# A gated linear attention with a feed-forward block on one core: the written-out order of five instruction queues is replaced by another

## The chip, the cores and the metric

One core of a Trainium2 chip runs the whole program in one launch. The metric is device time in microseconds (us), the median of several runs of the same program. TensorE (PE), VectorE (DVE), ScalarE (ACT), GpSimd (POOL) and SyncE (SP) each work through a queue of their own in order; an instruction whose inputs are not there yet holds up everything behind it on its engine. SP does no arithmetic here: it only issues DMA transfers. POOL computes and issues DMA transfers too.

## The reference

Inputs q, k, v and f_logit are float32, (4 batches, 8 heads, 768 tokens, 48). For each batch and head a 48x48 state is carried over the tokens:

```
f = 1 / (1 + exp(-f_logit))
state = f[t][:, None] * state + outer(k[t], v[t])
y[t]  = q[t] @ state
```

Then, with x = y as 3072 tokens x 384: h = x @ w_in (384 x 2048), g = 0.5 * (h + sqrt(h*h + 4)), out = g @ w_out (2048 x 384).

## The kernel before, in words

The 3072 tokens are cut into 24 **rows** of 128 tokens (r0 to r23; six rows a batch), and two rows make a **pair** (p0 to p11). Pairs 0 to 2 are loaded and prepared row by row (`FINE`), the others pair by pair. Each piece of work is an operation (`P.add`) with a letter in `TAKE` and a queue name in `NAME`:

- **Loads (SP, L315):** F, Q, K, V bring f_logit, q, k, v of a row (192 KB, one DMA) or of a pair (two DMAs).
- **Weights (POOL, L339):** w_in in eight parts, w_out in eight parts (192 KB each), in the order 0 to 7.
- **Logarithms (`add_logs`):** ACT takes exp (L360) and ln (L365) of F; "hi" (L368) and "lo" (L371) split the result into two fp16 tiles, on DVE or POOL.
- **Decays (`add_decays`):** PE makes the cumulative sums ("W", L402 to L409) in PSUM tiles `hps`; ACT takes ea and eap (L416); "q-mul" and "k-mul" (L422) give the decayed q and k, "v" (L429) is a cast, each on DVE or POOL; nls (L436, L438, DVE) and gam (L475, ACT) give the row's total decay.
- **Attention (`add_attention`), row by row:** q and k are transposed, for rows 0 to 9 on PE (T, L524) with a copy by DVE or ACT (L528), from row 10 on by a DMA transpose that SP issues ("xq", L512). Then the scores (SC, L549), the mask on DVE (pm, L556), the state (KV, L634 and L637, its copy sn on DVE, L641), the output (Y, L570 and L572), its copy (Yc, L579 on ACT or L581 on DVE), and the transpose of y into xT, on PE for rows 0 to 9 (YT, L614, L617) and by DMA from row 10 on ("xy", L604).
- **Feed-forward (`add_mlp1`, `add_mlp2`), pair by pair:** M1 (L671) is an eighth of h for one pair: six matmuls into one `hps` tile, for which both xT halves and one w_in part are needed; M1 of pair 6, part 3 is written M1 6.3. ACT squares it (L677) and takes one root for two parts (L686); DVE makes g (L694). M2 (L713) is a quarter of one row's output: four matmuls. The output tile is copied ("ev", L722 on ACT, L724 on DVE) and stored ("out", L728) from POOL or SP.

**What sets the order.** `TAKE` holds one string for each engine: the order in which that engine takes from its queues (each queue in its own order). `ENG` says, place by place, which engine does the operations that two engines can do: D for DVE, P for POOL, A for ACT, S for SP. `Plan.run` only merges the five strings into one program order. So the strings fix the whole schedule on each engine, and a wait at the head of a queue is a wait for all behind it.

Buffers that bind: five PSUM tiles `hps` (`NH`), shared in turn by M1, W and, in the first rows, attention. So an M1 part can't start before the g of the part five tiles back has been made. ACT changes its function table between the exp/ln work and the root (L761, L763), 12 loads in all. Load buffers: three for F, four each for Q, K, V.

Of the kernel before, what the change touches and what calls it, by code (L numbers as in the profile page):

```python
# [23 lines left out]
}  # L24
TAKE = {
    "PE":
        "WWTSTWSWYKTSYTKtStKYWYWttT11SK1K1Y1111T1t1S11211Y1t11122W2112222TT2K11S222YWW2t21S22T1TY22t2K11S112K"
        "1Y1Kt1122WS22WS22YY2t2K11S112YK22K211112S211211Y211S2112Y2WSW2KY2222S111KY12K222S112112YK112S112S11Y"
        "2211Y22SW2W22211212KY1K2211S211YK211S1122Y11S11K2222Y111S12222Y11211222111122221112122222222222",
    "ACT":  # L30
        "WWWWWWWWWWTWWWWWWWWcWWWWcWWWWWWmWmrmmrmmrmmrmmrmmrmmrmmrmmrWWWWWWWmmrmmrWWWWmWWWWWmrmmrmmrmcmrmmrWWW"
        "WWWWWmWmrmmrmmrmmrmmrmmrmmrmmrWWWWWWWWWmWmrmmrmmrmmrcmmrmmermmcrmmcrWWWWmWmrmmremmrmmrcmmrmmremmmmrr"
        "cemmmmrrecmmrmmrmmrmmremmmrmreee",
    "DVE":
        "hlvknnlSTSSnKnkSThSSTKStKStcckknntTtKSSggcKgghggTtgSggSggcgtgggggegkenTTlKhSSgggegckntnSSTeTcthKggSg"
        "SKggegKgtgggSSeSSccntKneSScKgggeKggSggSgggcegSgSggcgSSecgnKnSSeKKcggeggSSggKggSSgSggSgggeggSSknenKcg"
        "gKgSSgggKggSSggcggSKSggggSSgggggggeggggggggg",
    "POOL":
        "hlkkkhhvlvkkkvhiivlliiiiikkviuuuluuuuuvkholookkhvvolklkovvkoohkkhoollkkkkvhoohvlvlkkkovoo",
    "SP":  # L40
        "VFFFQHQVHFVQHHHFQFHVQQVVFQFFVVHHFFQQQVFHHHFqqVVHHqyyQqQQqqyFFyVqoqyVyqVqQHoyyQoqHqyyooVqyqyoyyoooo",
}

ENG = {
    "hi": "DPPPDPDPPPDPDPPPPPPPPPP",
    "lo": "DPDPPPPPDPPPPPPPPPPPPPP",
    "qk": "PPPDPPPDDDPPDPPPDPPPPPPPPPPPPPPPPPPPPPPPDPPPPP",
    "v16": "DPPPPPPPPPPPPPPPPPPPPPP",
    "T": "ADDDDDDDDDDDDDDDDDDDDDDD",
    "Yc": "AADDDDDDADDDDDDDAAADADAA",  # L50
    "ev": "DDDDDDDDDDDDADDAAAADAAAA",
    "out": "PPPPPPPPPSPPSSSSPSPSSSPS",
}
FULL = {"D": "DVE", "A": "ACT", "P": "POOL", "S": "SP"}

# [740 lines left out]
```

## Time and profile before

| | |
|---|---|
| median of 10 runs | 206.4 us (205.77 to 208.27) |
| profiled execution: device time, span | 206.07 us, 204.0 us |
| busy: PE, ACT, DVE, POOL | 179.9, 167.9, 140.9, 91.1 us |
| first M1 (0.0), last part of pair 0 (0.7), last M2 starts | 32.44, 43.26, 199.71 us |
| DMA traffic | 32.09 MB, mean 157 GB/s; about 190 GB/s in the first 20 us |
| largest waits listed for POOL | a store for an output copy (3 times, 37.5 us), the v cast for its load (3, 11.1 us), q-mul for its load (2, 9.7 us) |

Times inside a run count from the span's first instruction. The 2.07 us between span and device time lie outside the program's own instructions. A row of a timeline reads: start, duration, engine, line, operation, output and inputs, how many in a row, and in brackets the engine's idle time before it with what ended that. "SPq" is a DMA issue on SP. The profile gives the landing time of each DMA, which is later than its issue.

### The profile page before, as it was taken

Reading aid. Unit: us, or ns where it says so; the run is one execution under the profiler, and the core shown is the slowest. Engines: PE = TensorE matmul, PEld = TensorE weight load, DVE = VectorE, ACT = ScalarE, POOL = GpSimd, SP = SyncE. Lnnn points to the kernel's source line nnn. Section 1 sums busy time; section 2 is a strip of 40 time slices with the busy share of each in tenths; the row PEclk is TensorE's granted clock in tenths of the full one; section 3 lists DMA queues with packets and bytes.
Section 4 is the critical chain, followed back from the end, with each engine's and each line's share of the span. In section 5 each row is a group of like instructions: output and inputs, shape, how many; then the busy total and the mean of one; then the engine's idle time right before and its main releaser. Section 6 shows DMA issues by size and latency. Waiting matters only on the chain.

```text
span 204.0 us, 4839 instructions
## 1 busy us (share of the span) xinstructions
PE 179.9 (88%) x1870; PEld 131.4 (64%) x1870; DVE 140.9 (69%) x286; ACT 167.9 (82%) x271; POOL 91.1 (45%) x102
## 2 busy tenths in 40 slices
PE   0476869569999899999999998999999999999993
PEld 0243647457767577767777766677777776777751
DVE  5257655789768887987778974788665887465340
ACT  2674416989999999999989998899989997898840
POOL 6556489663045269629318779254061202010000
PEclk9999999999999999999999999999999999999998
DMA  6999999999999999989999799899709873221112
GB/s 118 190 192 187 165 179 217 191 184 208 186 194 216 206 223 176 202 171 224 166 157 169 180 178 203 177 184 181 174 26 195 156 142 63 59 58 42 39 39 77
DMA packets 128182, 32.09 MB, mean 157 GB/s; under 512 B 121088, under 2 KB 127488, under 8 KB 128160
## 3 DMA queue, kind: packets, MB, share of 16 engines
q1 hardware_dynamic: 121888, 25.90, 73.7%
q0 software_dynamic: 6272, 5.90, 14.8%
q8 instruction: 14, 0.23, 0.5%
q14 instruction: 8, 0.07, 0.1%
HBM read 25.17 MB, written 4.72 MB: 147 GB/s over the span
## 4 chain that ended last, share of the span: by engine, by line
PE 54%; ACT 17%; SPq 9%; DMA 9%; POOL 5%; issue 3%; DVE 1%; ACTq 0%; POOLq 0%
PE o L713 23%; PE hps L671 22%; SPq L315 9%; ACT hsq L677 5%; ACT r L686 5%; DMA w_in<-in_moe_w_in_dram 3%; DMA xT<-y 3%; POOL w_in L339 3%; DMA ld_v<-in_v_dram 2%; PE sc L549 2%; ACT ld_f L360 2%; PE y L572 1%; ACT L763 1%; ACT L761 1%; PE hps L402 1%
## 5 line engine op out<-in xcount | busy, mean ns | idle before, releaser
L694 DVE SCALAR_TENSOR_TENSOR g<-hps,r 128x512 f16<-128x512 f32 x96 | 62.7, 685 | 18.0 <-ACT r L686 17.5
L671 PE MATMUL hps<-xT,w_in 128*128 128x256 f16 x576 | 71.8, 273 | 3.5 <-DMA w_in<-in_moe_w_in_dram 2.5
L713 PE MATMUL o<-w_out,g 128*128 128x384 f16 x384 | 70.9, 326 | 0.0
L671 PEld LDWEIGHTS <-w_in 128*128 128x128 f16 x576 | 54.0, 98 | 13.5 <-DMA w_in<-in_moe_w_in_dram 3.3
L677 ACT ACTIVATE hsq<-hps 128x512 f16<-128x512 f32 x96 | 54.4, 593 | 7.3 <-PE hps L671 6.1
L686 ACT ACTIVATE r<-hsq 128x1024 f16<-128x1024 f16 x48 | 50.6, 1058 | 1.1
L713 PEld LDWEIGHTS <-g 128*128 128x128 f16 x384 | 35.6, 98 | 19.4
L556 DVE TENSOR_TENSOR pm<-sc,mask 128x512 f16<-128x512 f32 x48 | 31.6, 684 | 5.9 <-PE sc L549 5.8
L728 POOL DMA_DIRECT2D out_dram<-o_sb x14 | 7.9, 568 | 45.4 <-ACT o_sb L722 37.5
L422 POOL TENSOR_TENSOR qk<-ld_k,eap 128x768 f16<-128x768 f32 (+1 forms) x12 | 19.6, 1630 | 16.3 <-ACT eap L416 9.5
L422 POOL TENSOR_TENSOR qk<-ld_q,ea 128x768 f16<-128x768 f32 (+1 forms) x11 | 15.9, 1445 | 18.1 <-DMA ld_q<-in_q_dram 9.7
L371 POOL TENSOR_TENSOR llo<-ls,lhi 128x768 f16<-128x768 f32 (+1 forms) x12 | 16.7, 1401 | 6.2 <-DVE lhi L368 6.1
L641 DVE TENSOR_TENSOR sn<-u,gam 128x384 f16<-128x384 f32 x20 | 11.1, 553 | 11.4 <-PE u L637 7.0
L416 ACT ACTIVATE ea<-hps 128x384 f32<-128x384 f32 x24 | 10.9, 500 | 9.0 <-PE hps L409 8.8
L360 ACT ACTIVATE ld_f<-ld_f 128x768 f32<-128x768 f32 (+1 forms) x15 | 10.9, 725 | 8.3 <-DMA ld_f<-in_f_logit_dram 8.3
L429 POOL CAST v<-ld_v 128x768 f16<-128x768 f32 (+1 forms) x14 | 10.3, 736 | 14.4 <-DMA ld_v<-in_v_dram 11.1
L402 PE MATMUL hps<-lhi,wcent 128*128 128x384 f16 x24 | 8.8, 369 | 7.6 <-DVE lhi L368 6.9
L549 PE MATMUL sc<-qkT 48*128 48x128 f16 x192 | 10.6, 233 | 2.9 <-ACT qkT L528 1.1
L572 PE MATMUL y<-v,pm 128*128 128x48 f16 x192 | 12.0, 190 | 0.0
L365 ACT ACTIVATE ls<-ld_f 128x768 f32<-128x768 f32 (+1 forms) x15 | 10.8, 717 | 0.9
L581 DVE CAST y<-y 128x384 f16<-128x384 f32 x15 | 8.2, 552 | 4.4 <-PE y L572 4.2
L549 PEld LDWEIGHTS <-qkT 48*128 48x128 f16 x192 | 6.1, 99 | 8.0 <-issue 4.7
(55 smaller groups left out, 210.2 us busy)
## 6 DMA issues: line engine op xcount, KB each, us to landing
ld_v<-in_v_dram SPq DMA_DIRECT2D x24, 192.0 KB, 4.4
ld_f<-in_f_logit_dram SPq DMA_DIRECT2D x24, 192.0 KB, 4.6
ld_q<-in_q_dram SPq DMA_DIRECT2D x24, 192.0 KB, 4.2
ld_k<-in_k_dram SPq DMA_DIRECT2D x24, 192.0 KB, 4.5
out_dram<-o_sb POOLq DMA_DIRECT2D x14, 192.0 KB, 3.4
out_dram<-o_sb SPq DMA_DIRECT2D x10, 192.0 KB, 2.0
w_in<-in_moe_w_in_dram POOLq DMA_DIRECT2D x8, 192.0 KB, 6.1
w_out<-in_moe_w_out_dram POOLq DMA_DIRECT2D x8, 192.0 KB, 7.6
```

The source lines that it names most:

```text
L315: (nc.gpsimd if cast else nc.sync).dma_start(out=T["v16" if cast else name, p][:, r], in_=src_of[name][b][:, c * C:(c + 1) * C, :].rearran ...
L360: nc.scalar.activation(out=f, in_=f, func=AF.Exp, scale=-1.0)
L371: eng_of[lg[p, x].eng].tensor_tensor(out=llo[p % NL][:, x:y, :, 0:D], in0=T["ls", p][:, x:y], in1=lhi[p % NL][:, x:y, :, 0:D], op=ALU.subt ...
L422: eng_of[mu[p, x, i].eng].tensor_tensor(out=qk[p % NB][:, x:y, i, :, 0:D], in0=T[name, p][:, x:y], in1=T[e, p][:, x:y], op=ALU.mult)
L549: nc.tensor.matmul(out=T["sc", r, s][:, j, :], lhsT=qkT[o:o + D, NP + j, :], rhs=qkT[o:o + D, j, :], start=True, stop=True)
L556: nc.vector.tensor_tensor(out=T["pm", r][:, s], in0=T["sc", r, s], in1=mask16.unsqueeze(1).broadcast_to([128, NP, C]), op=ALU.mult)
L572: nc.tensor.matmul(out=y[:, j, s], lhsT=T["pm", r][:, s, j, :], rhs=T["v16", p][:, i, 2 * j + s, :], start=(c == 0), stop=(c == 0 or s == 1))
L671: nc.tensor.matmul(out=hb[:, a, :], lhsT=w_in16[j2][:, j, a * 128:(a + 1) * 128], rhs=T["xT", p][:, j, :], start=(j == 0), stop=(j == NJ - 1))
L677: nc.scalar.activation(out=T["hsq", p, j4][:, a], in_=T["h", p, j2], func=AF.Square, scale=1.0)
L686: nc.scalar.activation(out=T["r16", p, j4], in_=T["hsq", p, j4], func=AF.Sqrt, scale=0.25, bias=1.0)
L694: nc.vector.scalar_tensor_tensor(out=T["g", p][:, jn:jn + 2, :].rearrange("p a t -> p (a t)"), in0=T["h", p, 2 * j4 + a], scalar=0.5, in1= ...
L713: nc.tensor.matmul(out=T["o", p, i], lhsT=T["g", p][:, jn, i * C:(i + 1) * C], rhs=w_out16[jn // 2][:, jn % 2, :], start=(jn == 0), stop=( ...
```

## The change

Only the strings of `TAKE` and of `ENG` change. No operation, size, buffer or type does; the same 295 operations stand in PE's string, 96 M1 and 96 M2 parts among them.

```
 TAKE = {
     "PE":
-        "WWTSTWSWYKTSYTKtStKYWYWttT11SK1K1Y1111T1t1S11211Y1t11122W2112222TT2K11S222YWW2t21S22T1TY22t2K11S112K"
-        "1Y1Kt1122WS22WS22YY2t2K11S112YK22K211112S211211Y211S2112Y2WSW2KY2222S111KY12K222S112112YK112S112S11Y"
-        "2211Y22SW2W22211212KY1K2211S211YK211S1122Y11S11K2222Y111S12222Y11211222111122221112122222222222",
+        "WWTSKWWTYSTtKTYSKSWWYtYtt1T1SKY11Kt11T11S1111Y11t112112W2212221T21KT21222SW22YW2t2S12TT2Y1Kt21S1K112"
+        "Y11211Kt22WS2WS22YY2t2K11S121Y22K11K21121S12112Y11S211Y22WS2W2YK121222S12K2YK122S11211YK2112S112S112"
+        "11Y22Y2WWS222211Y122K12K211S121YK211S11221Y12S211K2Y21S1122122Y11112222111122221111222222222222",
     "ACT":
-        "WWWWWWWWWWTWWWWWWWWcWWWWcWWWWWWmWmrmmrmmrmmrmmrmmrmmrmmrmmrWWWWWWWmmrmmrWWWWmWWWWWmrmmrmmrmcmrmmrWWW"
-        "WWWWWmWmrmmrmmrmmrmmrmmrmmrmmrWWWWWWWWWmWmrmmrmmrmmrcmmrmmermmcrmmcrWWWWmWmrmmremmrmmrcmmrmmremmmmrr"
-        "cemmmmrrecmmrmmrmmrmmremmmrmreee",
+        "WWWWWWWWWWWWWWWWWTWWcWWWTTcWWWWcWmmWWrcmmrmmrmmrmmrmmrmmrmmrmmrWWWWWWWmmrmmrWWWWWWWWWmmrmmrmmrmmrmmr"
+        "WWWWWWWWWmmrmmrmmrmmrmmrmmrmmremmrWWWWWWWWWWmmrmmrmmrmmrcmmrmmrmmrmmrWWWWemWmrmmremmrmmrcmmrmmremmrm"
+        "mrcmmrmmrcmmmrmremmrmmrmmmrmree",
     "DVE":
-        "hlvknnlSTSSnKnkSThSSTKStKStcckknntTtKSSggcKgghggTtgSggSggcgtgggggegkenTTlKhSSgggegckntnSSTeTcthKggSg"
-        "SKggegKgtgggSSeSSccntKneSScKgggeKggSggSgggcegSgSggcgSSecgnKnSSeKKcggeggSSggKggSSgSggSgggeggSSknenKcg"
-        "gKgSSgggKggSSggcggSKSggggSSgggggggeggggggggg",
+        "hlkknnhThSlkkKSnnvkStSKSSKSScntnttvTSSKggtKgTgggSgSgggcggtgggggenkgTeThKggeSSggcktneSSnTTctKSggSggeg"
+        "KcggKtgggSSeSSnccntKeSScgKgggegKggSgSgcggSSggcgggSSnenKceSSKkcKggegSSggKgggSSggeggSSgcgggceSSnvknckK"
+        "gKggSSggKgggSgScggSSgggKegSSgggeggggggggggegggge",
     "POOL":
-        "hlkkkhhvlvkkkvhiivlliiiiikkviuuuluuuuuvkholookkhvvolklkovvkoohkkhoollkkkkvhoohvlvlkkkovoo",
+        "hlklvkvvkhhilliiikkiiikkihuuluvuuuuukovhollkhohvlokkvolkkkholvvhooklokkovvokhohollkkovooooo",
     "SP":
-        "VFFFQHQVHFVQHHHFQFHVQQVVFQFFVVHHFFQQQVFHHHFqqVVHHqyyQqQQqqyFFyVqoqyVyqVqQHoyyQoqHqyyooVqyqyoyyoooo",
+        "FFVVQQFHFFHVHQHVFQQVVHQFHHVQFFQFFFHHHVQVQQqqFVVqqyHyHFHQqqyyFVqyVQqyVqqQyVyHQyqqooHyyoqqyyoyo",
 }
 
 ENG = {
-    "hi": "DPPPDPDPPPDPDPPPPPPPPPP",
-    "lo": "DPDPPPPPDPPPPPPPPPPPPPP",
-    "qk": "PPPDPPPDDDPPDPPPDPPPPPPPPPPPPPPPPPPPPPPPDPPPPP",
-    "v16": "DPPPPPPPPPPPPPPPPPPPPPP",
-    "T": "ADDDDDDDDDDDDDDDDDDDDDDD",
-    "Yc": "AADDDDDDADDDDDDDAAADADAA",
-    "ev": "DDDDDDDDDDDDADDAAAADAAAA",
-    "out": "PPPPPPPPPSPPSSSSPSPSSSPS",
+    "hi": "PDDDPPPPDPPPPPPPPPPPPPP",
+    "lo": "PDPDPPPPPPPPPPPPPPPPPPP",
+    "qk": "DDPDDPPDPPPPPDPPDPPPPPPPPPPPPPPPPPPPPDPPPDPPDP",
+    "v16": "PPPDDPPPPPPPPPPPPPPPDPP",
+    "T": "DAAADDDDDDDDDDDDDDDDDDDD",
+    "Yc": "AADAADDDDDDDDDDDADDDADAA",
+    "ev": "DDDDDDDDADDDDDAAADDADADA",
+    "out": "PPPPPPPPPPPPPSSSPPSPPPPS",
 }
```

Read as operations, the first part of two queues, before and after ("F:r0" is the load of f_logit of row 0, "q*" and "k*" are q-mul and k-mul, "win0" is the first w_in part):

```
SP before  V:r0 F:r0 F:r1 F:r2 Q:r0 K:r0 Q:r1 V:r1 K:r1 F:r3 V:r2 Q:r2 K:r2 K:r3 K:r4 F:r4 Q:r3 F:r5 K:r5 V:r3 Q:r4 Q:r5 V:r4 V:r5 F:p3 Q:p3 F:p4 F:p5 V:p3 V:p4 K:p3
SP after   F:r0 F:r1 V:r0 V:r1 Q:r0 Q:r1 F:r2 K:r0 F:r3 F:r4 K:r1 V:r2 K:r2 Q:r2 K:r3 V:r3 F:r5 Q:r3 Q:r4 V:r4 V:r5 K:r4 Q:r5 F:p3 K:r5 K:p3 V:p3 Q:p3 F:p4 F:p5 Q:p4
POOL before hi:r1 lo:r1 q*:r0 k*:r0 q*:r1 hi:r2 hi:r3 v:r1 lo:r3 v:r2 q*:r2 k*:r2 q*:r3 v:r3 hi:r5 win0 win1 v:r4 lo:r4 lo:r5 win2 .. win6 q*:r5 k*:r5 v:r5 win7
POOL after  hi:r0 lo:r0 q*:r1 lo:r2 v:r0 k*:r2 v:r1 v:r2 q*:r3 hi:r4 hi:r5 win0 lo:r4 lo:r5 win1 win2 win3 q*:r4 k*:r4 win4 win5 win6 q*:r5 k*:r5 win7
```

PE around the first part of pair 6, and SP just before it:

```
PE before  W:p8 SC:14 W:p9 M2 9.3 KV:14 Y:14 M2 10.0 10.1 10.2 10.3 SC:15 M1 6.0 6.1 6.2 KV:15 Y:15 M1 6.3
PE after   W:p8 SC:14 M2 9.2 W:p9 M2 9.3 Y:14 KV:14 M1 6.0 M2 10.0 M1 6.1 M2 10.1 10.2 10.3 SC:15 M1 6.2
SP before  xq14 xq15 xy12 F:p10 F:p11 xy13 V:p8 xq16
SP after   F:p10 K:p9 Q:p8 xq14 xq15 xy12 xy13 F:p11 V:p8 xq16 xy14 V:p9 Q:p9 xq17 xy15 V:p10 xq18
```

By count: DVE does 19 of the hi, lo, q-mul, k-mul and v operations after (16 before); ACT does 3 of the copies behind T (1 before), 8 of the copies of y (9 before) and 7 of the output copies (9 before); 19 of the 24 stores leave from POOL (14 before). The number of ACT table loads stays 12.

## Prediction

> **What bounds the kernel now.** I read the busy time by stretch first, cut where the chain of waits changes character: 43.26 (last part of pair 0's M1), 85.72 (M1 3.7) and 200.54 (last M2 done).
>
> ```profile
> core 0: us, PE busy (x) PEld busy (x) DVE busy (x) ACT busy (x) POOL busy (x), PEclk, DMA share, GB/s
> 0.00:43.26 43.26, 25.56 (x275) 18.01 (x275) 26.13 (x68) 24.91 (x47) 28.08 (x46) 1.00 1.17 180
> 43.26:85.72 42.46, 40.55 (x434) 30.04 (x435) 34.31 (x67) 40.80 (x65) 23.17 (x22) 1.00 1.16 202
> 85.72:200.54 114.82, 113.80 (x1164) 83.37 (x1161) 80.42 (x153) 101.68 (x160) 39.87 (x35) 1.00 0.71 135
> 200.54:204.00 3.46, 0.00 (x0) 0.00 (x0) 0.00 (x0) 0.48 (x1) 0.00 (x0) 0.85 0.16 57
> ```
>
> PE's work is the same before and after, so only its idle time can change: 17.7 us before 43.26, 1.9 us up to 85.72, 1.0 us up to 200.54, and 3.5 us for the last copy and store. In the middle stretch ACT is as full as PE; in the last one PE alone is.
>
> Next, what ends the first stretch. PE's timeline and POOL's:
>
> ```profile
> 39.87 0.83 PE L671 MATMUL hps<-xT,w_in 128*128 128x256 f16 x6 [0.77 <-DMA w_in<-in_moe_w_in_dram]
> 41.67 0.83 PE L671 MATMUL hps<-xT,w_in 128*128 128x256 f16 x6 [0.97 <-DMA w_in<-in_moe_w_in_dram]
> 43.26 0.83 PE L671 MATMUL hps<-xT,w_in 128*128 128x256 f16 x6 [0.76 <-DMA w_in<-in_moe_w_in_dram]
> ```
>
> ```profile
> 20.86 1.00 POOL L422 TENSOR_TENSOR qk<-ld_q,ea 128x384 f16<-128x384 f32 x1 [2.12 <-DMA ld_q<-in_q_dram]
> 24.37 0.50 POOL L429 CAST v<-ld_v 128x384 f16<-128x384 f32 x1 [2.52 <-DMA ld_v<-in_v_dram]
> ...
> 25.27 1.71 POOL L339 DMA_DIRECT2D w_in<-in_moe_w_in_dram  x2
> 27.68 0.50 POOL L429 CAST v<-ld_v 128x384 f16<-128x384 f32 x1 [0.70 <-DMA ld_v<-in_v_dram]
> ...
> 29.88 3.87 POOL L339 DMA_DIRECT2D w_in<-in_moe_w_in_dram  x5
> ```
>
> The last w_in parts end PE's waits, and they are issued by POOL behind casts and products that wait for loads. Last, the one real PE wait after 85.72, in the chain of waits and in SP's timeline:
>
> ```profile
> 118.65 5.51 DMA xT<-y
> 124.20 2.12 PE hps L671 x18
> ```
>
> ```profile
> 115.66 2.90 SPq L315 DMA_DIRECT2D ld_f<-in_f_logit_dram  x4
> 118.65 2.12 SPq L604 DMA_TRANSPOSE xT<-y  x1
> ```
>
> M1 6.0 waits 1.00 us for the transposed y of row 13, issued behind four F DMAs.
>
> **The change part by part.** The sum is made against the profiled execution, 206.07 us (span 204.0 and 2.07 around it); the median, 206.4, is 0.33 above.
>
> *A. The start (0 to 44).* In the trace the loads land about 1.04 us apart whatever they carry (14th at 17.59, 18th at 22.69, 26th at 33.0), so I give each place in SP's new order the landing of that place before. On POOL everything up to the first weight now ends with the q-mul of row 3, whose load Q:r3 is the 18th: 22.7. From there POOL's rows add up: q-mul 1.00 and two hi of 0.51 put the first weight at 24.7 (25.27 before). That weight, 0.85, and two lo of 0.91 put the second at 27.4 (26.19 before); the third leaves at 28.2 (29.88 before); then two more of 0.78, q-mul and k-mul of row 4 at 1.00 each, three weights, q-mul and k-mul of row 5: the eighth leaves at 36.1, against 36.12 before. So the last weight is issued when it was. But its landing was set by the stream as well: the last four landed 1.6 to 2.1 us apart (37.75, 39.83, 41.63, 43.21), though three of them had been issued 0.78 apart. With the third and fourth weight 1.7 us earlier, the last lands between 1.6 us earlier and no earlier. I take **-0.8**, the middle; on the bad side +2.5 (the third rival).
> The attention rows start later: the mask of row 0 (pm, second half) now stands on DVE behind the q-mul of row 2, which waits for Q:r2, the 14th load, 17.59; so Y:0 comes near 19.4 instead of 16.95. It is caught up, since the W of rows 4 and 5 no longer wait for lo behind v casts (W:r4 stood 1.80 us, until 29.1; lo:r4 is now done at 26.5). M1 0.0 then comes at 31 to 32.4 (32.44 before), and the weights are the later anyway. The two T copies that ACT takes over (1.01 each) lie where ACT is idle for 18 of 43 us. T:5 and YT:4 move ahead of M1 0.7 (0.45 + 0.17 of PE work), which I cost at nothing gained: behind them M1 2.1 waits for g 1.4 and so for ACT's roots in either order.
>
> *B. 43 to 86.* ACT has no idle time from 44.12 to 96.44, so it sets how fast PSUM tiles come free. M1 3.7 needs the tile of g 3.2, done at 84.90, and started at 85.72: no more than 0.8 is to be had. Two waits go or shrink:
>
> ```profile
> 61.24 0.84 PE L524 MATMUL tr<-ident,qk 128*128 128x128 f16 x12 [0.50 <-POOL qk L422]
> ...
> 69.05 0.32 PE L402 MATMUL hps<-lhi,wcent 128*128 128x384 f16 x1 [0.69 <-DVE g L694]
> ```
>
> T:6 waited for the k-mul of pair 3 on POOL (1.81); it is now on DVE (0.95), the q-mul on POOL beside it. The W of pair 5 now stands behind M2 3.0, 3.1 and Y:6, 1.7 us of work, so its tile is free. Against that, Y:6 comes right after its masks, which stand on DVE behind two g and an output copy (+0.5 at the worst). I take **-0.5**; bounds -0.8 and +0.5.
> DVE's row beside this: the cast hi of row 4 took 1.00 us on DVE (21.07 to 22.07) while POOL's q-mul ran (20.86 to 21.85); the cast of the same shape for row 0 took 0.36 alone. The Trainium skill (SBUF — State Buffer, "Who interferes with whom") says that a DVE instruction with two SBUF inputs and a GpSimd one that reads SBUF shut each other out, the later one wholly. It speaks against the change, which gives DVE 19 such operations instead of 16: by it, an estimate, pair 3's two products would run one after the other, 1.81 + 0.95 from 58.3, until 61.1, as late as before, and B would be -0.2.
>
> *C. M1 6.0.* The y transpose of row 13 (xy13) now goes out right behind xy12, ahead of the F loads of pair 11; pair 10's stand well ahead of it. Y:13 comes earlier in PE's order too, and its copy was done at 116.24 already before. From 116.3, with the page's 3.0 us median to landing, xT is there at 119.3; with the 5.5 it took before, at 121.8. PE would have reached M1 6.0 at 123.2; now four M2 (4 x 0.65) and SC:15 (0.33) stand behind it instead of ahead: 120.3. So the wait goes, **-1.0**; at the worst it is 1.5 instead of 1.0, +0.5. Late next: M1 6.5 needs g 6.0, which ended at 130.32, and started at 131.54: 1.2 us of room, enough for 1.0. ACT behind it is full (103.1 to 124.5); it gains one output copy there (ev:8, 0.48) and loses its 0.55 us idle at 103.13.
>
> *D. New waits.* Three places have little room, on the clock of before. (1) The load Q of pair 9 goes from place 55 of SP's queue to 65. It now stands behind xq16 (its k-mul ended at 122.21), xy14 and V of pair 9, 1.2 to 1.3 us each by SP's rows: issued near 126 instead of 106.43, landed five us later as then (111.51), so near 131.5; 1.81 for its q-mul on POOL and 4.0 for xq18 as before (131.04 to 135.09) make 137.5. SC:18 stood at 139.80, less what the rest gains. (2) xq22 stands behind xy20, whose y copy comes after the root of M1 8.7 (ended at 162.92): 0.46 for the copy, 1.2 for xy20, 0.4 for a store and 3.7 for xq22 (161.68 to 165.42) make 168.7; SC:22 stood at 168.52 and moves back by 0.5. (3) On POOL the lo of pairs 10 and 11 stand behind the store of row 12: M2 12.3 ended at 139.7, copy and store 1.1, two lo of 1.64: 144.1; W of pair 11 stood at 148.07 and moves 1.2 forward. The room is 0.3 to 2.8 us, by rows that scatter by about as much. I take **+0.5** in all; bounds 0 and +2.
>
> Moves at no cost: the five stores that go from SP to POOL (0.57 each) are covered by POOL's idle time, 75 of 115 us after 85.72; the output copies that go from ACT to DVE (0.55) by DVE's 34 idle us there. Without that cover each would cost its own length once. The end does not change: the last M2, a copy on ACT, a store from SP, 3.5 us.
>
> Sum: 206.07 - 0.8 - 0.5 - 1.0 + 0.5 = 204.3 profiled, and 0.33 more as a median: **204.6**.
>
> **The rivals.**
> *Same, 206.0.* The weights land as before, since the last is issued at the same time (A 0). ACT sets the pace of the middle (B 0). The wait of M1 6.0 goes (-1.0), and D gives 0.6 back: 206.4 - 0.4. For it: ACT's 40.80 of 42.46. Against it: 2.5 us of POOL issues are earlier.
> *Slower, 207.9.* One mechanism: POOL's line ahead of the eighth weight. The k-mul of row 5 stands right before it, and its load K:r5 falls from place 19 (landed 23.58) to place 25, behind both F DMAs of pair 3 and beside the weights. If it lands as the 26th DMA did, 33.0, there are 2.1 us to spare before 35.1. But a load beside the weights can take far longer: F:p4 was issued at 31.89 and landed at 44.79. From 35.1 on each us costs one us at M1 0.7 and at the end; past 36.1 it has eaten B, C and D together (-1.0). With K:r5 at 37.6, A is +2.5: 206.4 + 2.5 - 1.0 = 207.9.
> *The order doesn't reach the chip as written* has no weight: the listing of the built program shows it on each engine.
>
> **How the numbers follow.** Forecast 0.50, same 0.20, slower 0.30. A difference under 0.5% (1.0 us) can't be told from none here; the bounds are 205.4 and 207.4. All of the forecast's bounds at their best (A -1.6, B -0.8, C -1.0, D 0) give 203.0; the slower rival reaches 207.9. Range 202.9 to 207.9, with the forecast's own from 203.0 to 205.4. Faster 0.50, same 0.20, slower 0.30.
>
> **What would show it.** A: the last wait of M1 0.7 for w_in, its start between 41.6 and 43.3; later than 44.3 and the slower rival holds, with the k-mul of row 5 waiting for ld_k. B: M1 3.7 between 0.3 and 1.0 earlier than A alone makes it. C: no wait for xT at M1 6.0 (M1 7.0 and 8.0 likewise). D: waits of SC:18, SC:22 and W:p11. The forecast is wrong if PE's idle time after M1 0.7 is over 3 us, or if M1 0.7 is late.

## The result, and the profile after

The changed kernel takes 204.0 us (median of 14 runs, 202.79 to 207.02), the kernel before 206.33 us beside it (median of 51): a ratio of 0.9885, 95% interval 0.9861 to 0.9908. The ratios here and below leave out the runs counted as slow, those more than 1.5% above the fastest of their kernel, and are not the quotients of the two medians. The same kernel measured once more gave 203.59 us against 206.06, ratio 0.9894 (0.9845 to 0.9942). The forecast was 204.6 us.

The profiled execution took 203.24 us, its span is 201.5 us: 2.5 us less span than before. It lies 0.76 us below the median of its kernel, while the one of before lay 0.26 below its own (206.33); so of the 2.83 us between the two profiled executions only 2.3 are there in the medians. How far runs with a start like this one's differ is the subject of the last experiments.

The busy time by stretch, after, cut at the times of before except for the last cut, which lies 0.33 us behind the end of the last M2 (197.67):

```profile
core 0: us, PE busy (x) PEld busy (x) DVE busy (x) ACT busy (x) POOL busy (x), PEclk, DMA share, GB/s
0.00:43.26 43.26, 25.45 (x299) 18.39 (x299) 27.45 (x69) 27.88 (x52) 29.24 (x46) 1.00 1.25 180
43.26:85.72 42.46, 41.27 (x430) 29.79 (x425) 32.80 (x63) 41.59 (x65) 24.31 (x23) 1.00 1.10 199
85.72:198.00 112.28, 111.95 (x1151) 82.19 (x1149) 83.79 (x159) 98.92 (x155) 37.44 (x36) 1.00 0.72 140
198.00:201.50 3.50, 0.00 (x0) 0.00 (x0) 0.00 (x0) 0.23 (x1) 0.00 (x0) 0.89 0.16 56
```

PE's idle time in the middle stretch fell from 1.9 to 1.2 us, in the long one from 1.0 to nothing: the 0.3 that its row shows lies behind the last M2. From the end of the last M2 to the end of the span it is 3.8 us (3.5 before). The first stretch reads nearly the same as before, because its cut stands still while the work moved: M1 0.7 now starts at 42.29 instead of 43.26, so 0.97 us more of later work lies inside it. Its PEclk of 1.00 can't be taken as it reads: the trace holds no granted clock before 26.67 us (32.27 before), and PE's rows ahead of that are slow (eight transposes take 1.01 us at 15.88, 0.61 at 39.20).

PE's timeline of the start, after (the same view as before's three rows of M1 behind w_in parts):

```profile
35.45 0.20 PE L570 MATMUL y<-sn,qkT 128*128 128x96 f16 x1 [1.56 <-DVE sn L641]
...
40.01 0.83 PE L671 MATMUL hps<-xT,w_in 128*128 128x256 f16 x6 [0.20 <-DMA w_in<-in_moe_w_in_dram]
42.29 0.83 PE L671 MATMUL hps<-xT,w_in 128*128 128x256 f16 x6 [1.45 <-DMA w_in<-in_moe_w_in_dram]
```

The last w_in part still ends M1 0.7's wait, but there is a wait of another kind ahead: the output of row 4 (Y:4) waits 1.56 us for the state copy sn, and M1 0.2 and 0.3 stand behind it in PE's order. POOL's timeline shows what the eighth weight stood behind:

```profile
33.02 1.01 POOL L422 TENSOR_TENSOR qk<-ld_q,ea 128x384 f16<-128x384 f32 x1
35.67 1.00 POOL L422 TENSOR_TENSOR qk<-ld_k,eap 128x384 f16<-128x384 f32 x1 [1.64 <-DMA ld_k<-in_k_dram]
36.61 0.80 POOL L339 DMA_DIRECT2D w_in<-in_moe_w_in_dram  x1
```

The load K:r5 landed at 35.53. That is the wait that the slower rival named, and it is there: 1.64 us. And M1 6.0, in SP's and PE's timelines:

```profile
112.40 2.71 SPq L604 DMA_TRANSPOSE xT<-y  x2
115.20 1.16 SPq L315 DMA_DIRECT2D ld_f<-in_f_logit_dram  x2
```

```profile
118.33 0.82 PE L671 MATMUL hps<-xT,w_in 128*128 128x256 f16 x6
```

xy12 and xy13 go out together ahead of F:p11, xy13 lands at 116.31, and M1 6.0 has no bracket: it waits for nothing.

Where the time went, as starts on PE after minus before, each less what was gained ahead of it: M1 0.7 -0.97; from there to M1 3.7 another -0.60; from there to the last M2 another -1.28 (all but 0.1 of it at M1 6.0). Behind the last M2 0.33 is given back, so that the span is 2.52 shorter, and the time outside the span is 0.3 less.

### The profile page after: what moved, and what is told of

It reads as the page before. It is cut to its first block, busy times and chain, and to the rows that moved or that the text cites. A ratio compares the mean times of both kernels' runs of the same rounds, so it can differ in the third digit from the quotient of the medians.

```text
span 201.5 us, 4841 instructions
## 1 busy us (share of the span) xinstructions
PE 178.7 (89%) x1870; PEld 130.4 (65%) x1870; DVE 144.0 (71%) x290; ACT 168.6 (84%) x270; POOL 91.0 (45%) x104
## 4 chain that ended last, share of the span: by engine, by line
PE 59%; DMA 13%; SPq 11%; ACT 8%; POOL 4%; issue 2%; DVE 0%; POOLq 0%; ACTq 0%
PE o L713 25%; PE hps L671 23%; SPq L315 11%; DMA ld_k<-in_k_dram 7%; DMA w_in<-in_moe_w_in_dram 3%; ACT hsq L677 3%; PE sc L549 2%; DMA ld_f<-in_f_logit_dram 2%; ACT r L686 2%; DMA ld_q<-in_q_dram 2%; POOL llo L371 2%; PE y L572 2%; PE y L570 1%; PE u L637 1%; PE hps L402 1%
## 5 line engine op out<-in xcount | busy, mean ns | idle before, releaser
L671 PE MATMUL hps<-xT,w_in 128*128 128x256 f16 x576 | 73.4, 273 | 3.1 <-DMA w_in<-in_moe_w_in_dram 2.8
L713 PE MATMUL o<-w_out,g 128*128 128x384 f16 x384 | 71.9, 326 | 0.0
L728 POOL DMA_DIRECT2D out_dram<-o_sb x19 | 10.7, 564 | 44.7 <-DVE o_sb L724 20.1
L422 POOL TENSOR_TENSOR qk<-ld_q,ea 128x768 f16<-128x768 f32 (+1 forms) x11 | 16.7, 1519 | 28.3 <-ACT ea L416 22.0
L422 POOL TENSOR_TENSOR qk<-ld_k,eap 128x768 f16<-128x768 f32 (+1 forms) x9 | 14.2, 1578 | 19.3 <-PE hps L671 11.5
L371 POOL TENSOR_TENSOR llo<-ls,lhi 128x768 f16<-128x768 f32 (+1 forms) x13 | 18.4, 1425 | 3.3 <-DVE lhi L368 3.1
L724 DVE COPY o_sb<-o 128x384 f32<-128x384 f32 x17 | 9.4, 553 | 6.2 <-PE o L713 6.2
L572 PEld LDWEIGHTS <-pm 128*128 128x128 f16 x192 | 10.1, 99 | 5.5 <-DVE pm L556 2.8
L524 PE MATMUL tr<-ident,qk 128*128 128x128 f16 x80 | 8.1, 255 | 4.3 <-DVE qk L422 3.7
L429 POOL CAST v<-ld_v 128x768 f16<-128x768 f32 (+1 forms) x12 | 9.0, 758 | 6.3 <-DMA ld_v<-in_v_dram 6.3
```

Of the source, the lines that this page charges most:

```text
L371: eng_of[lg[p, x].eng].tensor_tensor(out=llo[p % NL][:, x:y, :, 0:D], in0=T["ls", p][:, x:y], in1=lhi[p % NL][:, x:y, :, 0:D], op=ALU.subt ...
L422: eng_of[mu[p, x, i].eng].tensor_tensor(out=qk[p % NB][:, x:y, i, :, 0:D], in0=T[name, p][:, x:y], in1=T[e, p][:, x:y], op=ALU.mult)
L572: nc.tensor.matmul(out=y[:, j, s], lhsT=T["pm", r][:, s, j, :], rhs=T["v16", p][:, i, 2 * j + s, :], start=(c == 0), stop=(c == 0 or s == 1))
L671: nc.tensor.matmul(out=hb[:, a, :], lhsT=w_in16[j2][:, j, a * 128:(a + 1) * 128], rhs=T["xT", p][:, j, :], start=(j == 0), stop=(j == NJ - 1))
L713: nc.tensor.matmul(out=T["o", p, i], lhsT=T["g", p][:, jn, i * C:(i + 1) * C], rhs=w_out16[jn // 2][:, jn % 2, :], start=(jn == 0), stop=( ...
```

## The experiments

The traces are compared by two numbers: when M1 0.7 starts, and how long after it the last M2 starts (156.45 us before, 154.57 after). My theory was that of the forecast: three separate terms (the start, the middle, M1 6.0). The first rival was that the orders work only together, the second that K:r5 in front of the eighth weight decides.

### The two halves of the change: start_of_after and rest_of_after

Cut at 43.3 us: one kernel takes the new order for the operations that start before it in either kernel, the other for the rest.

```
 start_of_after   SP  FFVVQQFHFFHVHQHVFQQVVHQFHHVQFF (after) + VHFFQQQVFHHHFqqVV... (before)
 rest_of_after    SP  VFFFQHQVHFVQHHHFQFHVQQVVFQFFV (before) + HQFFFHHHVQVQQqqFV... (after)
```

> All operations that either kernel starts before 43.3 us stand in the order (and on the engines) of the changed kernel, the rest as in the kernel before. Theory (the stretches are separate terms): M1 0.7 starts near 42.3 instead of 43.26, the middle and the end go as before, the wait of M1 6.0 for xT is still there; time 1.0 us under before, ratio 0.995. Rival (the start's gain is taken back by ACT's pace unless the later order is changed too): M1 0.7 early, but M1 3.7 within 0.4 us of before; ratio 0.998 to 1.000.

> The opposite half: the start as in the kernel before, everything that both start after 43.3 us as in the changed kernel. Theory (separate terms): M1 0.7 at 43.3, M1 3.7 0.6 us and M1 6.4 1.9 us earlier than before; time 1.9 us under before, ratio 0.991. Rival (the later order needs the early start to have its loads and weights in time): new waits in the middle, ratio 0.995 or more.

Measured: the start alone 205.19 us, ratio 0.9967 (0.9936 to 0.9998); the rest alone 206.68 us, ratio 1.0033 (1.0007 to 1.0059). Multiplied, the two ratios give 1.0000, the whole change 0.9885: the halves do not add. One trace for each half shows where.

The start alone brings M1 0.7 to 42.78 (-0.47), and the interval of its ratio holds the 0.995 of the theory. Its profiled execution then loses 2.5 us at M1 6.0, but it is the longest of its twelve, 208.05 us, and the others (203.84 to 206.47) have no profile: it shows what can happen, not what the start alone costs. PE's timeline there, and the windows around it:

```profile
122.39 0.40 PE L549 MATMUL sc<-qkT 48*128 48x128 f16 x8
124.69 3.35 PE L671 MATMUL hps<-xT,w_in 128*128 128x256 f16 x18 [1.90 <-DMA xT<-y]
```

```profile
core 0: us, PE busy (x) PEld busy (x) DVE busy (x) ACT busy (x) POOL busy (x), PEclk, DMA share, GB/s
...
122.40:124.69 2.29, 0.39 (x9) 0.31 (x9) 1.75 (x3) 0.99 (x2) 2.29 (x2) 1.00 1.20 89
124.69:126.69 2.00, 2.00 (x13) 1.57 (x13) 0.00 (x0) 1.87 (x5) 0.64 (x1) 0.68 1.34 202
126.69:128.69 2.00, 2.00 (x16) 1.46 (x15) 0.00 (x0) 1.94 (x5) 1.78 (x3) 0.50 1.10 262
```

The wait for the transposed y of row 13 is 1.90 us instead of 1.00: PE comes 0.41 earlier, and the transpose lands 0.49 later (124.65 against 124.16). And behind it the granted clock falls to 0.68 and 0.50, so that the 18 matmuls of M1 6.0 to 6.2, 2.12 us before, take 3.35. A gain ahead of a wait that stays is taken back there, in this execution with interest.

The rest alone, with the start of before, has M1 0.7 at 44.10 and M1 2.1 2.07 us late: T:5 now stands directly behind M1 0.7, and SC:5 waits 0.62 for its copy. SP runs late as well, and two transposes have no room: M1 5.0 waits 0.71 us for xT and SC:18 0.18 us for qkT. From M1 2.1 to the end it still gains 0.78. So in its trace the later order does worse behind the start of before. The first rival holds for this later half, which was to give 0.991; for the start the measured ratio fits either. The places of the three terms were right.

### The transpose of row 13 by itself: xy13_first and xy13_first_f10_early

In the kernel before, on SP only:

```
 before                SP  ... xq14 xq15 xy12 F:p10 F:p11 xy13 V:p8 ...
 xy13_first            SP  ... xq14 xq15 xy12 xy13 F:p10 F:p11 V:p8 ...
 xy13_first_f10_early  SP  ... F:p10 xq14 xq15 xy12 xy13 F:p11 V:p8 ...
```

> The kernel before with one move in SP's queue: xy13 ahead of the F loads of pairs 10 and 11 instead of behind them. Theory A (the place of xy13 alone made M1 6.0 wait): the wait for xT goes, 1.0 us under before, ratio 0.995. Theory B (the F load of pair 10 has no time to give: it landed at 120.53 and its exp started at 120.65): exp of pair 10 waits 1 us or more on ACT, the root of pair 6 and g 6.0 come as much later, and M1 6.5 waits in place of M1 6.0: ratio 0.998 to 1.002.

> As the run with xy13 first, and the F load of pair 10 moved up ahead of xq14, as in the changed kernel. Theories A and B both: neither M1 6.0 nor the exp of pair 10 waits, 1.0 us under before, ratio 0.995. If it is no faster, something else than the two places on SP holds pair 6 back (ACT's full stretch 103 to 124.5).

Measured: xy13_first 206.84 us, ratio 1.0051 (1.0028 to 1.0073), slower. The wait at M1 6.0 does go (its start is 1.11 earlier). But ACT and PE in that kernel:

```profile
122.20 0.85 ACT L360 ACTIVATE ld_f<-ld_f 128x768 f32<-128x768 f32 x1 [1.39 <-DMA ld_f<-in_f_logit_dram]
...
125.63 0.84 ACT L360 ACTIVATE ld_f<-ld_f 128x768 f32<-128x768 f32 x1 [1.65 <-DMA ld_f<-in_f_logit_dram]
```

```profile
128.37 0.32 PE L634 MATMUL u<-sn,ident 128*128 128x384 f16 x1 [1.13 <-DVE sn L641]
```

F:p10 lands at 122.11 and F:p11 at 125.55 (120.53 and 122.19 before). ACT takes their exponentials at a place where it had no idle time, the decay of row 16 (gam) stands behind them on ACT, the state copy behind that on DVE, and KV:16 on PE. The end comes 1.55 us later. With F:p10 ahead of xq14 as well, as the change has it, M1 6.0 starts 1.00 us earlier and every row behind it 0.98; the profiled span is 203.0. The timing doesn't settle it: 205.29 us against 206.06, ratio 0.9993 (0.9959 to 1.0026). So the term C is worth 1.0 in the trace, by two moves and not by one: F:p10 had to be out of the way first.

### The load ahead of the eighth weight: k5_late, win7_early, win7_and_k5_early

In the changed kernel:

```
 after                SP    ... Q:r5 F:p3 K:r5 K:p3 V:p3      POOL ... win6 q*:r5 k*:r5 win7
 k5_late              SP    ... Q:r5 F:p3 V:p3 K:r5 K:p3      POOL as after
 win7_early           SP    as after                          POOL ... win6 win7 q*:r5 k*:r5
 win7_and_k5_early    SP    ... Q:r5 K:r5 F:p3 K:p3 V:p3      POOL ... win6 win7 q*:r5 k*:r5
```

> The changed kernel, and on SP alone the load V of pair 3 put ahead of K of row 5, so that K of row 5 is issued one load later. It tests the price of the slower rival (past 35.1 on the clock of before each us of the k-mul of row 5 costs one at M1 0.7 and at the end). In the changed kernel K:r5 landed at 35.53, the k-mul began at 35.67 and ended at 36.67, the eighth weight left at 36.61 and M1 0.7 started at 42.29. Theory A (POOL's line sets the last weight, one for one): K:r5 lands 1 to 5 us later, the eighth weight leaves that much later, and M1 0.7 and the end go back by the same, so that the end is 1 to 5 us later than the changed kernel's 203.24 profiled. Theory B (the stream of the weights sets it, the k-mul has room behind it): M1 0.7 goes back by less than half of what the k-mul does, and the end by under 1 us.

> The changed kernel, and on POOL alone the eighth weight put directly behind the seventh, ahead of the q-mul and k-mul of row 5 (K:r5 landed at 35.53 and made the weight wait until 36.61). Theory A (the wait for K:r5 costs what it shows): the eighth weight leaves near 33.0 instead of 36.6, and as the weights then land 1.5 us apart, as the others do, it lands at 41.5 instead of 42.24: M1 0.7 starts 0.7 earlier than 42.29 and the end comes 0.5 to 0.8 earlier. Theory B (the stream is full in any case, and the eighth weight in it only delays the loads beside it): M1 0.7 within 0.2 us of 42.29, K:r5 lands later than 35.53, and the end is the same or later.

> Both: the eighth weight directly behind the seventh on POOL, and the load K of row 5 ahead of F of pair 3 on SP. Theory A (both are terms of their own): M1 0.7 0.7 to 1.2 us earlier than 42.29, the end 0.6 to 1.2 earlier than the changed kernel. Theory B (what the weights win, the roots on ACT or the loads F of pair 3 give back): M1 0.7 0.5 earlier or more, but M1 3.7 by less than half of that, and the end within 0.3 us of the changed kernel's 203.24 profiled.

k5_late (four runs): 209.61 us, ratio 1.0198 (1.0143 to 1.0253). K:r5 lands at 40.80, 5.27 later; POOL and PE:

```profile
40.94 1.00 POOL L422 TENSOR_TENSOR qk<-ld_k,eap 128x384 f16<-128x384 f32 x1 [6.87 <-DMA ld_k<-in_k_dram]
41.87 0.80 POOL L339 DMA_DIRECT2D w_in<-in_moe_w_in_dram  x1
```

```profile
46.09 1.25 PE L671 MATMUL hps<-xT,w_in 128*128 128x256 f16 x5 [3.05 <-DMA w_in<-in_moe_w_in_dram]
```

The weight leaves 5.26 later and M1 0.7 starts 3.80 later: the first 1.5 us of the delay cost nothing there. The end is 5.91 later, because the wait of 3.05 us halves PE's clock (the first five matmuls of M1 0.7 take 1.25 us; all six took 0.83 after), which costs another 1.1 up to M1 2.1, and because 1.0 more is lost between M1 6.4 and M1 7.0, for a cause that stays open. The rival's mechanism is real: 5.91 us at the end for 5.27 at the load is no less than the 1 for 1 that it asked, though at M1 0.7 it is 3.80; one place on SP separates the changed kernel from it.

win7_early: 205.24 us, ratio 0.9960 (0.9921 to 0.9999), no better than the changed kernel. The eighth weight leaves at 33.00 instead of 36.61, and lands at 42.67; in five executions with the start unchanged it landed at 42.24 to 43.37. So 3.6 us of issue show no gain: the fifth to eighth weights land at 38.30, 39.54, 41.14 and 42.67, 1.2 to 1.6 apart, and the 1.64 us of waiting on POOL cost the changed kernel nothing that this execution shows. It is one execution: its fifth weight, issued as in the changed kernel (30.66 against 30.62), landed 1.33 later, so the 0.7 of theory A isn't excluded. SP's loads land later in it: V:p3 at 52.54 instead of 45.40, Q:p3 at 55.06 instead of 51.42 (one kernel below, with the weight in its old place, has V:p3 at 50.59, so the early weight needn't be the cause). SP is late from there on, and at the far end:

```profile
105.22 0.81 PE L671 MATMUL hps<-xT,w_in 128*128 128x256 f16 x6 [0.76 <-DMA xT<-y]
...
138.78 0.40 PE L549 MATMUL sc<-qkT 48*128 48x128 f16 x8 [0.41 <-DMA qkT<-qk]
```

M1 5.0 and SC:18 wait for their transposes, the end is 1.4 us further from M1 0.7 than in the changed kernel. SC:18 is the first of the three places that the forecast's term D named.

win7_and_k5_early: 207.39 us, ratio 1.0073 (1.0044 to 1.0103): slower than before. K:r5 lands at 30.54, nothing waits on POOL, the eighth weight is there at 41.72. But F:p3 comes one place later, at 35.59 instead of 31.75. One row each of ACT, DVE and PE:

```profile
35.67 0.84 ACT L360 ACTIVATE ld_f<-ld_f 128x768 f32<-128x768 f32 x1 [5.56 <-DMA ld_f<-in_f_logit_dram]
```

```profile
38.56 0.56 DVE L641 TENSOR_TENSOR sn<-u,gam 128x384 f16<-128x384 f32 x1 [4.37 <-ACT gam L475]
```

```profile
39.17 0.24 PE L570 MATMUL y<-sn,qkT 128*128 128x96 f16 x1 [5.86 <-DVE sn L641]
...
39.80 2.73 PE L671 MATMUL hps<-xT,w_in 128*128 128x256 f16 x12
```

The exponential of pair 3 waits for F:p3, the decay of rows 4 and 5 stands behind it on ACT, the state copy sn:4 behind that on DVE, Y:4 behind that on PE, and M1 0.2 behind Y:4. M1 0.7 starts at 45.51, 3.2 late, without a wait for any weight. This chain into M1 0.7 is the one that the forecast didn't have. In the changed kernel it is the 1.56 us ahead of Y:4. With no wait between, M1 0.6 starts 3.71 us behind M1 0.2 (35.31 to 39.02 in v5_later, below) and M1 0.7 could 0.65 later; from 35.82 that gives 40.2, against 42.29 for the weights: 2.1 us of room. Here M1 0.2 came 3.98 later, and the wait of 5.86 halved PE's clock on top: the 12 matmuls of M1 0.2 and 0.3 take 2.73 us instead of 1.47.

### Both products of pair 3 on DVE: p3_both_dve

```
-POOL  ... wout7 q*:p3 out:0 v:p3 ...      DVE ... ev:0 nls:p3 k*:p3 g:2.1 ...
+POOL  ... wout7 out:0 v:p3 ...            DVE ... ev:0 q*:p3 nls:p3 k*:p3 g:2.1 ...
```

> The changed kernel with the q-mul of pair 3 on DVE too, right ahead of its k-mul (in the changed kernel the q-mul ran on POOL from 57.44 to 59.25 and the k-mul on DVE from 58.30 to 60.06, 1.76 long where k-muls of this shape take 0.95 alone). Theory A (the two shut each other out): the k-mul takes 0.9 to 1.0 again, T:6 (transposes of pair 3) starts no later than in the changed kernel, or up to 0.6 earlier, though DVE has 0.95 more to do. M1 3.7 and the end move by less than 0.4 us either way, since g 3.2 and ACT's roots set them. Theory B (the k-mul was long for another cause): it takes 1.7 or more again, T:6 comes 0.9 later, and the end by 0.2 to 0.9.

Measured: 204.19 us, ratio 0.9929 (0.9902 to 0.9957); in the trace M1 0.7 starts at 42.73, the last M2 154.51 behind it (154.57 after). In the changed kernel, DVE and POOL:

```profile
58.30 1.77 DVE L422 TENSOR_TENSOR qk<-ld_k,eap 128x768 f16<-128x768 f32 x1
```

```profile
57.44 1.81 POOL L422 TENSOR_TENSOR qk<-ld_q,ea 128x768 f16<-128x768 f32 x1 [11.44 <-ACT ea L416]
```

With both on DVE, and POOL's cast of v beside them:

```profile
57.80 1.82 DVE L422 TENSOR_TENSOR qk<-ld_q,ea 128x768 f16<-128x768 f32 x1 [0.72 <-ACT ea L416]
...
59.81 0.96 DVE L422 TENSOR_TENSOR qk<-ld_k,eap 128x768 f16<-128x768 f32 x1
```

```profile
57.96 0.84 POOL L429 CAST v<-ld_v 128x768 f16<-128x768 f32 x1
```

The k-mul takes 0.96 as soon as POOL has nothing beside it, and 1.77 while POOL's q-mul runs (0.81 more; POOL's q-mul went on for the first 0.95 of it). Now the q-mul is the long one, 1.82, beside a cast of 0.84 on POOL: 0.96 + 0.84 is 1.80. So DVE's product is longer by about as long as POOL reads beside it; theory A holds. This is the rule of the Trainium skill that the forecast weighed (SBUF — State Buffer, "Who interferes with whom"), and the two runs agree with it in that the two don't run at once. That the later one waits they don't show: in the second, DVE's row starts 0.16 ahead of the cast and is still the long one. The second half of theory A was wrong: T:6's second half starts 18.09 us behind M1 0.7 instead of 17.83, so DVE alone is no faster than both. And it doesn't matter: the end moves by 0.06.

### W of pair 5 in its old place: w5_back

```
-PE  ... W:p4 M2 3.0 M2 3.1 Y:6 W:p5 M2 3.2 ...
+PE  ... W:p4 W:p5 M2 3.0 M2 3.1 Y:6 M2 3.2 ...
```

> The changed kernel, and on PE alone W of pair 5 put back directly behind W of pair 4, where it waited 0.69 for the g of 2.4 in the kernel before. Theory A (that wait was the term B): W:p5 waits 0.5 to 1.0 again, M1 3.7 starts 0.3 to 0.7 later relative to M1 0.7 than the 41.86 of the changed kernel, and the end is 0.3 to 0.7 later. Theory B (ACT's roots set the pace of the stretch, and PE's waits in it are only where its slack shows): the wait comes back, but M1 3.7 stands within 0.2 of 41.86 behind M1 0.7.

Measured: 206.52 us, ratio 1.0017 (0.9986 to 1.0048). The wait is back, in the middle of W:p5, and longer than the 0.69 before:

```profile
70.79 0.32 PE L402 MATMUL hps<-lhi,wcent 128*128 128x384 f16 x1 [1.36 <-DVE g L694]
```

M1 3.7 starts 43.82 us behind M1 0.7 instead of 41.86, and the last M2 156.52 instead of 154.57: 1.95 us. Of that 0.28 stood already at M1 1.3, ahead of the move; some 1.7 are left for the move, more than twice the most that theory A asked. M1 2.6 comes 2.33 later against M1 0.7, and ACT's work behind it with it. In the changed order the place of W:p5 matters to the middle stretch; 0.28 us more of T:6's wait, in the experiment before this one, cost nothing. The rest of the 206.52 lies ahead of M1 0.7, which started at 43.95 although this kernel's orders up to there are those of the changed one.

### How steady is the start: after_again

The changed kernel once more.

> The changed kernel itself, once more. Three kernels with the same orders up to M1 0.7 started it at 42.29 (the changed kernel), 42.73 (both products of pair 3 on DVE) and 43.95 (W of pair 5 put back); with the start of before it came at 42.98, 43.26 and 43.34. Theory A (the orders set it, and the term A of the forecast is steady): M1 0.7 within 0.4 of 42.29, F of pair 3 lands within 0.5 of 31.75, the ratio to before lies between 0.985 and 0.991. Theory B (with the new order F of pair 3 and K of row 5 land among the weights, and how they share the engines differs from one execution to the next): M1 0.7 anywhere from 42.2 to 44.0 and the last M2 154.6 behind it within 0.3, whatever it is; the single times spread over 2 us, and the ratio is 0.986 to 0.996.

Measured: 203.59 us (203.27 to 205.24), ratio 0.9894 (0.9845 to 0.9942). M1 0.7 starts at 42.95, the last M2 154.49 behind it. The two halves belong into the comparison too, since their orders up to M1 0.7 are those of the changed kernel and of before. So five executions with the same start have M1 0.7 at 42.29, 42.73, 42.78, 42.95 and 43.95; four with the start of before at 42.98, 43.26, 43.34 and 44.10. Theory B holds for the start: 42.95 and the landing of F:p3, 32.43, lie outside theory A's bounds; the ratio lies in both ranges. The five have F:p3 landing at 31.75, 31.95, 32.79, 32.43 and 33.73 and the eighth weight at 42.24, 42.68, 42.74, 42.91 and 43.37, the weight in the same sequence as M1 0.7. They were run on at least four chips, so whether a chip or a single execution sets the difference is not shown. In after_again, PE and the granted clock:

```profile
35.95 0.20 PE L570 MATMUL y<-sn,qkT 128*128 128x96 f16 x1 [2.34 <-DVE sn L641]
...
36.32 2.34 PE L671 MATMUL hps<-xT,w_in 128*128 128x256 f16 x12
```

```profile
core 0: us, PE busy (x) PEld busy (x) DVE busy (x) ACT busy (x) POOL busy (x), PEclk, DMA share, GB/s
...
36.00:38.00 2.00, 2.00 (x22) 1.61 (x22) 0.29 (x1) 1.99 (x4) 2.00 (x3) 0.69 1.41 198
38.00:40.00 2.00, 2.00 (x15) 1.55 (x13) 1.34 (x4) 1.81 (x4) 1.99 (x4) 0.50 1.33 224
```

Behind a wait of 2.34 us for sn:4 the clock goes to half, from 36.75 to 40.16: the 12 matmuls of M1 0.2 and 0.3 take 2.34 us where they took 1.47 behind the wait of 1.56. Here the last weight, landed at 42.91, still hid it. In w5_back, where the wait was 3.43, it did not: M1 0.7 waited for no weight there.

### A later load with room: v5_later, v5_later_f3_early

```
 after              SP  ... Q:r4 V:r4 V:r5 K:r4 Q:r5 F:p3 K:r5 K:p3 ...
 v5_later           SP  ... Q:r4 V:r4 K:r4 Q:r5 F:p3 K:r5 V:r5 K:p3 ...
 v5_later_f3_early  SP  ... Q:r4 V:r4 K:r4 F:p3 Q:r5 K:r5 V:r5 K:p3 ...
```

> The changed kernel, and on SP alone the load V of row 5 moved behind K of row 5, so that K of row 4, Q of row 5, F of pair 3 and K of row 5 each go out one load earlier. V:r5 has room: it landed at 25.68 and its cast ran at 41.98. Theory A (both chains into M1 0.7 get shorter: F:p3 to ACT to the state of row 4 to M1 0.2, and K:r5 to POOL to the eighth weight): K:r5 lands before 33.5, the wait of 1.64 goes, the eighth weight leaves near 35.0 instead of 36.61, M1 0.2 starts 1 earlier than 35.82, M1 0.7 0.5 to 1.0 earlier than 42.29, and the end 0.4 to 1.0 earlier than the changed kernel (profiled 202.2 to 202.9). Theory B (the order has no such slack: the weights and these loads share one stream, which is full): M1 0.7 within 0.4 of 42.29 (the scatter that unchanged starts showed: 42.29 and 42.73), the end within 0.5.

> The same, and F of pair 3 ahead of Q of row 5 too (Q:r5 landed at 29.73 and was used at 33.02). Theory A: F:p3 lands 2 us earlier than 31.75, so the exponential of pair 3 and the state of row 4 behind it come 2 earlier, M1 0.2 as soon as its weight is there (33.3 landed); M1 0.7 as in the run with V of row 5 moved alone, within 0.3, since the eighth weight sets it; the end 0.4 to 1.0 earlier than the changed kernel. Theory B: the end as late as the changed kernel's within 0.5, and the wait of the fourth row's state turns into waits for weights.

The profiled execution of v5_later is the shortest of the study, 202.49 us, span 200.7. K:r5 lands at 31.57, POOL waits for nothing, M1 0.2 starts at 35.31, 0.5 earlier, half of what theory A asked:

```profile
41.60 0.83 PE L671 MATMUL hps<-xT,w_in 128*128 128x256 f16 x6 [1.76 <-DMA w_in<-in_moe_w_in_dram]
```

M1 0.7 is 0.69 earlier than in the changed kernel and the last M2 154.50 behind it: theory A for the rest, in the trace. The twelve runs don't bear it out: they lie from 202.49 to 206.79, with a median of 205.67 us (before 205.95 beside it); the ratio, 0.9941 (0.9900 to 0.9982), is that of the five shortest, up to 205.12. The second kernel, 205.42 us, ratio 0.9979 (0.9948 to 1.0010), gains nothing measurable; its profiled execution took 363 us and is not read. I can't say that either beats the changed kernel, and whether the wait ahead of Y:4 grew past what halves the clock in the longer ones stays open: one of twelve was profiled.

## Why the forecast was right, step by step

The forecast, 204.6 us, was 0.6 above the median, inside its range, on the right side; the likeliest case came. Its four terms in the profiled execution:

| step | forecast | profiled | what the runs add |
|---|---|---|---|
| A, the start | -0.8 (-1.6 to +2.5) | -0.97 | second execution -0.31; mean of five starts against four -0.5 |
| B, middle | -0.5 (-0.8 to +0.5) | -0.60 | second execution -0.66 |
| C, M1 6.0 | -1.0 (to +0.5) | -1.28 | second execution -1.30; alone -1.06 |
| D, new waits | +0.5 (0 to +2) | 0 | 0 twice; 0.18, 0.41 and 0.16 at SC:18 in three kernels with other starts |

**A** had the right place, and the last weight still ended M1 0.7's wait. Its size for the median is uncertain: the five starts average 42.94 and the four of before 43.42, so of -0.8 some -0.5 is left, with a scatter of 1.7 and 1.1 us. Several steps in it failed. The loads were not 1.04 us apart throughout: that holds up to the 17th (20.72), from there to the 26th (33.0) they were 1.4 apart. The first weight left at 23.69 and not at 24.7, and M1 0.0 came at 29.51 and not at 31 or later. K:r5 was to land like the 26th DMA, at 33.0; it landed at 35.53, past the 35.1 from which the slower rival was to cost 1 us per us, and no cost shows. By k5_late the first 1.5 us behind that landing are free, so the price began near 37.0 and not at 35.1, and a landing at 37.6 would have cost some 0.6 and not 2.5 (an estimate from these two executions). So both the landing and the threshold were wrong, on opposite sides. And the moves on PE were said to cost nothing, by a look at T:5 and YT:4; what I didn't see is that Y:4 now stands ahead of M1 0.2, where it had stood ahead of M1 0.4, and that sn:4 hangs on F:p3. Nor is PE's work "the same" in time: its rows are slow until 32.27 before and until 26.67 after. M1 0.7 waited for a weight in both, so this decided nothing there.

**B**: of the two waits that were to go, W:p5's is gone and T:6's isn't:

```profile
60.12 0.40 PE L524 MATMUL tr<-ident,qk 128*128 128x128 f16 x4 [0.42 <-DVE qk L422]
...
68.59 0.32 PE L402 MATMUL hps<-lhi,wcent 128*128 128x384 f16 x1
```

T:6 waited 0.50 us before and waits 0.42 now. That the place of W:p5 matters is shown by w5_back, but not that it makes up the whole 0.60: a wait of 0.21 at Y:8 went as well. The value taken was right; the -0.2 that the skill's rule gave is not what came, though the rule itself holds, since the k-mul of pair 3 took 1.77 us instead of 0.96 beside the q-mul. The error in that estimate was to put T:6's wait on the path. Seven of the 19 operations on DVE that it counted are casts with one input, which the quoted rule doesn't name.

**C**: right in its place, its cause and nearly its size. The missing 0.28 is the 0.1 at M1 4.0 and the small gaps of PE in the long stretch. The forecast named the move of F:p10 in half a sentence; xy13_first shows that without it the end comes 1.55 later instead of 1.0 earlier.

**D** is the mis-sized term of the sum: +0.5 forecast, 0 measured. The arithmetic on the first place was good (Q:p9 issued at 124.12, landed at 129.19, xq18 at 136.35, SC:18 at 136.97: 0.6 us of room; the places of Q:p9 are 56 and 66, not 55 and 65). It is thin: three kernels (rest_of_after, win7_early, win7_and_k5_early) fell into it. The end did change, which the forecast said it wouldn't: +0.33 behind the last M2.

By these averages A gave some 0.3 less, C 0.3 more, and D took 0.5 less, which is most of the 0.6 by which the median lies under the forecast. That the errors of A and C cancel is luck. The rival "same" had A and B at nothing; B is not. The slower rival's mechanism exists, by k5_late, one load away.

What stays open: how often each start comes in the changed kernel (two executions of it were profiled), whether A is more than the scatter of the starts, and whether v5_later is faster.

## What to carry to other kernels

A wait that goes ahead of a wait that stays is not a gain: follow the next fixed point (a transpose, a load with its own queue) and ask whether it moves too; here the two halves of the change, measured alone, came to a ratio of 1.0000 multiplied, and the whole to 0.9885. Before a load is moved one place, list everything that hangs on its neighbours: K:r5, F:p3 and V:r5 stood side by side, the first fed the weights, the second the roots and the state, and only the third had room. And take the size of a gain among loads that share engines from several executions, not from one: the same orders put M1 0.7 anywhere within 1.7 us.

## What the runs showed of the hardware

PE's clock can halve with waits of under 2 us. Once it had been at 1.00, waits of 1.56, 1.76 and 1.89 us left it there; with waits of 1.80, 1.90, 2.06, 2.34, 2.67, 2.98, 3.05, 3.43 and 5.86 us it was at 0.50 for 3.4 us (twice that at 2.67, 3.43 and 5.86), each M1 part taking 1.3 us instead of 0.65. At the border a wait of 1.80 did (p3_both_dve) and one of 1.89 didn't (win7_early), so the length alone doesn't decide. The changes come in steps: in start_of_after the clock is at half from 36.66 to 40.08 and from 125.41 to 128.82, and these times lie whole multiples of 3.41 us apart, so it also matters how a wait lies in these steps. In start_of_after PE worked up to 1.90 us before M1 6.0 and right behind it, so the step before 125.41 was idle for 1.90 us and not throughout. The Trainium skill (TensorE: Matmul & The Clock Gate, "What's actually happening") gives a window of about 3.4 us that runs freely, and a clock at half after an idle one. The steps agree with such a window; that it has to be idle does not agree with these 1.90 us.

The weights land further apart than they leave: the last four 1.2 to 1.6 us apart after POOL had issued them 0.8 apart, and a weight issued 3.6 us sooner landed at 42.67, within the 42.24 to 43.37 of the unchanged starts (win7_early). The landing of one load in one order scatters by 2 us and more there: F:p3 from 31.75 to 33.73, V:p3 from 45.40 to 50.59.
